# Attention and gated FFN on one core: the order of the work at the end of a sequence and at the start of the kernel

## The chip, the cores and the metric

The kernel runs on one core of a Trainium2 chip. The metric is the device time of an execution in microseconds (us); runs are compared by their median. A core has a tensor engine (PE; its weight loads are shown apart, as PEld), a vector engine (DVE), a scalar engine (ACT), GpSimd (POOL) and a sync engine (SP) that here only starts DMA transfers. Each engine works through its own queue in order, and waits for the others by semaphores. PE writes its results to PSUM, which has eight banks; DVE and ACT read them from there. POOL works on SBUF alone.

## What is computed

Eight sequences (B) of 448 tokens with 12 heads (H) of 64. First attention with normed queries and keys, then a gated feed-forward network on the heads side by side (768 values a token). All data is float32; the weights arrive as float64.

```
q_n, k_n = rmsnorm(q, g_q), rmsnorm(k, g_k)
attn = softmax(q_n @ k_n.T / sqrt(64));  o = attn @ v
x = o, heads side by side: (8 * 448, 768)
xn = x / sqrt(mean(x * x) + 1e-6) * rms_g
out = (silu(xn @ w_gate) * (xn @ w_val)) @ w_out      # 768 -> 1536 -> 768
```

## The kernel before

**Pairs.** The function `safe_scores` works on pairs of heads: `g` counts 48 of them, six to a sequence `b`. The loop over `g` is at the end of the function. For a pair:

- `load_pair`, `load_v`: loads of q, k and v, on SP's queue.
- `squares(g, i)` (L424, L427): ACT squares q (i = 0) or k (i = 1), DVE sums the squares. `rms_qk` (L441, L444): POOL scales the sums `ms` and raises them to the power -1/2 (`rs`). `norm_q` (L448): POOL multiplies q by its `rs`, giving `qn`, a tile with one buffer.
- `turn(g, i)` (L461 to L466): PE transposes `qn` (i = 0) or k (i = 1); ACT brings the first to SBUF with the gains `gqk` as a scale, DVE the second (`qkT`). While the list of feed-forward steps is not empty, their bank is the single bank of `ps_m`.
- `score(g, (0, 1))` and `score(g, (2, 3))` (L476, L480): each fills four banks of `ps_s` (four there are) and ACT takes the exponential of each into `e`, with the key's `rs` as its scale.
- `values(g)` (L501): `e` times v into `av`, also in the `ps_m` bank. `sums(g)` (L512 to L533): the denominators `den`, their reciprocal `rd` on DVE, the product of both to `x`, the square of `x` on ACT, and its sum over the pairs of a sequence, `ss`, on POOL. For g up to 6 (`direct`) `den` is summed by PE from `e`; after that POOL adds the `e` first (L486, L490).

**The norm of a sequence.** `rms_x` sums `ss` over its partitions with PE (`msx`, L546), DVE scales it (L548), POOL takes the power (L550). `norm_x` spreads that power over all partitions with eight matmuls on PE (`rb`, L556), and DVE multiplies the six chunks of `x` by it and by the gain `rg` (L560). `left_factors` makes four sums and differences of quarters of `x` (S1 to S4, L571) for all sequences but the first.

**The feed-forward steps.** The gate and value products of a sequence are made with Strassen's scheme: `quad` does them in seven steps of 12 matmuls (L783), whose results DVE adds (L795), with a tanh on ACT (L802) and two operations on DVE that give `h` (L805, L806). A sum `so` over parts of `h` (L858 to L861) is made for the output product. The first sequence is multiplied plainly (L1008, L1017 to L1020). The output product is `project_out` (L878) for the first two sequences and `out_strassen` (L977) after that. `begin(b, slots)` puts the steps of the output product of sequence b - 1 and of the gate and value products of b into the list `todo`, and `fill` takes them from there between the attention steps of later pairs: a given number, or as many as the share of the slot asks for. Seven steps are left over for the end of the sequence.

**Conversion.** `convert` moves the float64 weights on by one stage each: load (L619), `split` on ACT (L628, L629), `join` on DVE (L634 to L636), one addition on POOL (L672), and a store to scratch memory (L660). It is called at fixed places of the loop and after each step of `fill`; 78 calls do all of it.

**The order.** The engines' queues are filled in the order in which the Python code runs; nothing reorders it. `pe(fn)` counts PE's steps, and `after(n, fn)` hands work to other engines n steps later; n = 0 is right behind the running step. The sum of `squares`, for example, is issued one step later and its power two (for pairs 0 and 1, one). At a sequence's end (`hp == 0`, from g = 12 on) the loop runs: three steps of `todo`, squares of pair g + 2, first turn of g + 1, one step, `rms_x`, one step, `norm_x`, one step, second turn, the rest of the list, `begin`.

Of the kernel before, what the change touches and what calls it, by code (L numbers as in the profile page):

```python
# [8 lines left out]
F32 = mybir.dt.float32  # L9
# [3 lines left out]
ALU = mybir.AluOpType  # L13
# [8 lines left out]
NPAIR = H // 2  # L22
# [3 lines left out]
HT = S // 2  # L26
# [308 lines left out]
def safe_scores(  # L335
# [20 lines left out]
    nc = tc.nc  # L356
# [5 lines left out]
    const, small = pool("c_const", 1), pool("c_small", 4)  # L362
# [5 lines left out]
    ps_s, ps_m, ps_f = pool("c_ps_s", 4, space=PSUM), pool("c_ps_m", 1, space=PSUM), pool("c_ps_f", 3, space=PSUM)  # L368
# [9 lines left out]
    def after(n, fn):  # L378
        due.append((now["t"] + n, fn))

    def pe(fn):
        now["t"] += 1
        fn()
        for item in [d for d in due if d[0] <= now["t"]]:
            due.remove(item)
            item[1]()
# [16 lines left out]
    def load_v(g):  # L403
        if g >= NG:
            return
        b, hp = divmod(g, NPAIR)
        vt = st["v", g] = v_pool.tile([P, 2, NT, D], F32, name="vt")
        nc.sync.dma_start(out=vt.rearrange("p h t d -> p h (t d)"),
                          in_=v[b, 2 * hp:2 * hp + 2].rearrange("h (p t) d -> p h (t d)", t=NT))
# [5 lines left out]
    def squares(g, i):  # L415

        if g >= NG:
            return
        n = 2 * NT
        if i == 0:  # L420
            st["ms", g] = small.tile([P, 2 * n], F32, name="ms")
        ms = st["ms", g]
        sq = tmp.tile([P, n * D], F32, name="sq", tag="sq", bufs=2)
        nc.scalar.activation(sq, st["qk", g][:, i], ACT.Square)  # L424

        def reduce():
            nc.vector.tensor_reduce(out=ms[:, i * n:(i + 1) * n], in_=sq.rearrange("p (n d) -> p n d", d=D), axis=AX_X, op=ALU.add)  # L427

        after(1, reduce)
        if g <= 1:  # L430

            after(1, lambda: rms_qk(g, slice(i * n, (i + 1) * n)))
            if i == 0:
                after(1, lambda: norm_q(g))
        elif i == 1:
            after(2, lambda: rms_qk(g))
            after(2, lambda: norm_q(g))
# [103 lines left out]
    def rms_x(b):  # L541
        assert st["summed", b] == NPAIR - 1
        ss = st.pop(("ss", b))
        ps = ps_f.tile([128, 512], F32, name="msx", tag="f")
        for t in range(NT):
            nc.tensor.matmul(ps[0:P, t:t + 1], lhsT=ss[:, t * P:(t + 1) * P], rhs=ones[:, 0:1], start=True, stop=True)  # L546
        ms = small.tile([P, NT], F32, name="ms4")
        nc.vector.tensor_scalar(ms, ps[0:P, 0:NT], 1.0 / DM, 1e-6, ALU.mult, ALU.add)  # L548
        rs = st["rx", b] = small.tile([P, NT], F32, name="rs4")
        nc.gpsimd.tensor_tensor(rs, ms, mhalf[0:P, 0:NT], ALU.pow)  # L550

    def norm_x(b):
        rs = st.pop(("rx", b))
        ps = ps_f.tile([128, 512], F32, name="rb", tag="f")
        for t in range(NT):
            nc.tensor.matmul(ps[:, t * P:(t + 1) * P], lhsT=rs[:, t:t + 1].to_broadcast([P, 128]), rhs=ident[0:P, 0:P],  # L556
                             start=True, stop=True)
        for hp in range(NPAIR):
            x = st["x", b, hp // 3][:, hp % 3, :]
            nc.vector.scalar_tensor_tensor(x, x, rg[:, hp:hp + 1], ps[:, 0:S], ALU.mult, ALU.mult)  # L560

    def left_factors(b):

        a = st["left", b] = {f"A{r + 1}{h + 1}": st["x", b, h][:, :, r * HT:(r + 1) * HT] for r in range(2) for h in range(2)}
        for h in range(2):
            st.pop(("x", b, h))

        def op(name, first, second, what):

            a[name] = a["A21"] if name == "S3" else s_pool.tile([128, 3, HT], F32, name="xs")  # L570
            nc.vector.tensor_tensor(a[name], a[first], a[second], what)  # L571

        op("S1", "A21", "A22", ALU.add)
        op("S2", "S1", "A11", ALU.subtract)
        op("S3", "A11", "A21", ALU.subtract)
        op("S4", "A12", "S2", ALU.subtract)

    NFP = NFC // 2

# [82 lines left out]
    def convert():  # L662

        n = turn_of["n"]
        if n >= TURNS or not room(1):
            return False
        turn_of["n"] += 1
        if 0 <= n - 4 < len(pieces):
            key = pieces[n - 4][0]
            st[key] = block()  # L670
            lo, top = st.pop(("cv", n - 4))
            nc.gpsimd.tensor_tensor(data(key).bitcast(I32), top, lo, ALU.add)  # L672
        if 0 <= n - 3 < len(pieces):
            st["cv", n - 3] = join(*st.pop(("cv", n - 3)))
        if 0 <= n - 2 < len(pieces):
            st["cv", n - 2] = split(st.pop(("raw", n - 2)))
        if n < len(pieces):
            st["raw", n] = load_raw(pieces[n][1])
        if 0 <= n - 6 < len(pieces):
            keep(pieces[n - 6][0])  # L680
        return True
# [384 lines left out]

    def begin(b, slots):

        if b:
            left_factors(b)  # L1070
        items = (out_items(b - 1) if b else []) + gate_value_items(b)
        part.update(all=float(sum(c for c, *_ in items[:-LEFT])), spent=0.0, slot=0, slots=slots)
        todo.extend(items + (out_items(b) if b == B - 1 else []))
# [14 lines left out]
    for a in range(2):  # L1088
        rows = slice(a * D, (a + 1) * D)
        nc.scalar.dma_start(out=gq[rows, :], in_=g_q.rearrange("(p o) -> p o", o=1))  # L1090
        nc.scalar.dma_start(out=gk[rows, :], in_=g_k.rearrange("(p o) -> p o", o=1))
    for g in range(2):
        load_v(g)
    rg = const.tile([128, NDC], F32, name="rg")
    nc.sync.dma_start(out=rg, in_=moe_rms_g.rearrange("(c p) -> p c", p=128))
    row = const.tile([1, 2, D], F32, name="row")
    nc.sync.dma_start(out=row[:, 0, :], in_=g_q.rearrange("(o d) -> o d", o=1))
    nc.sync.dma_start(out=row[:, 1, :], in_=g_k.rearrange("(o d) -> o d", o=1))
    gqk = const.tile([128, 1], F32, name="gqk")

    def bound():
        nc.vector.scalar_tensor_tensor(gqk, gq, 1.0 / D**0.5, gk, ALU.mult, ALU.mult)

        nc.vector.tensor_scalar(gqk, gqk, SAFE / D, -SAFE / D, ALU.min, ALU.max)
        nc.vector.tensor_tensor(row[:, 0, :], row[:, 0, :], row[:, 1, :], ALU.mult)
        top = const.tile([1, 1], F32, name="top")
        nc.vector.tensor_reduce(out=top, in_=row[:, 0, :], axis=AX_X, op=ALU.max, apply_absolute_value=True)
        nc.vector.tensor_scalar(flag, top, 8.0, SAFE, ALU.mult, ALU.is_gt)


    squares(0, 0)
    pe(idle)
    squares(0, 1)
    pe(lambda: turn(0, 1))
    convert()
    convert()
    bound()
    squares(1, 0)
    squares(1, 1)
    pe(lambda: turn(0, 0))  # L1120
    convert()
    for g in range(NG + 1):
        b, hp = divmod(g, NPAIR)
        load_pair(g + 2)
        if g <= NPAIR:
            pe(lambda: score(g, (0, 1)))
            squares(g + 2, 0)
            squares(g + 2, 1)
            convert()
            pe(lambda: turn(g + 1, 0))  # L1130
            pe(lambda: turn(g + 1, 1))
            if g:
                pe(lambda: values(g - 1))
            load_v(g + 2)
            convert()
            if g:
                pe(lambda: sums(g - 1))
            pe(lambda: score(g, (2, 3)))
            convert()
            continue  # L1140

        if g < NG:
            pe(lambda: score(g, (0, 1)))
        pe(lambda: values(g - 1))
        load_v(g + 2)
        if g == NPAIR + 1:
            pe(lambda: rms_x(0))
            pe(lambda: score(g, (2, 3)))
            pe(lambda: norm_x(0))
        pe(lambda: sums(g - 1))  # L1150
        if g == NPAIR + 1:
            begin(0, 15)
        elif g < NG:
            pe(lambda: score(g, (2, 3)))
        end = hp == 0
        fill(3 if end else None)
        squares(g + 2, 0)
        squares(g + 2, 1)
        pe(lambda: turn(g + 1, 0))
        if end:  # L1160
            fill(1)
            pe(lambda: rms_x(b - 1))
            fill(1)
            pe(lambda: norm_x(b - 1))
        fill(1 if end else None)
        pe(lambda: turn(g + 1, 1))
        if end:
            fill(len(todo))
            begin(b - 1, 16)
        fill()  # L1170
    fill(len(todo))
    for _ in range(3):
# [39 lines left out]
```

## Time and profile before

| | us |
|---|---|
| median of 11 runs (lowest to highest) | 1667.8 (1661.15 to 1669.77) |
| the profiled execution | 1666.87 |
| its span, first to last instruction | 1665.1 |
| PE busy in the span | 1625.8 |
| DVE / ACT / POOL busy | 854.9 / 499.6 / 627.9 |
| mean granted clock of PE | 0.991 |
| DMA traffic | 273.28 MB, 164 GB/s |

The profile is one execution. A line of its time line gives the start and the time of a run of like instructions, the engine, the line of code, the operation, what it writes and reads, and how often; in brackets stands the idle time before it and what ended it. Matmuls overlap, so a PE that is shown as busy may still run slowly; the granted clock tells how much of its full speed it was given. Each float32 matmul of the code is two instructions on PE, a transpose is one.

By the time line the first sequence's attention takes the first 95 us, its gate and value products follow up to about 265, and the seven ends of sequences with `norm_x` in the loop's last part lie at 257, 456, 669, 864, 1069, 1262 and 1460 us. (The first `norm_x`, at 97 us, has a branch of its own.)

### The profile page before, as it was taken

The numbers are of one execution on the slowest core, as the hardware profiler recorded it, in microseconds if no ns is written. First come the engines' busy times: TensorE is split into PE (matmuls) and PEld (weight loads), VectorE is DVE, ScalarE is ACT, GpSimd is POOL, SyncE is SP. The second block draws the span as 40 slices with busy tenths as digits, with TensorE's granted clock in tenths as the row PEclk, the third lists the DMA queues.
The fourth block names the chain that finished last, engine by engine and source line by source line (L and its number), as shares of the span: only waits on it lengthen the run. The fifth ranks groups of instructions, "written<-read, shape, count | busy, mean of one in ns | idle before, by whom it ended". The sixth has DMA issues, their size and how long they took to land.

```text
span 1665.1 us, 21470 instructions
## 1 busy us (share of the span) xinstructions
PE 1625.8 (98%) x7376; PEld 1148.1 (69%) x7376; DVE 854.9 (51%) x1371; ACT 499.6 (30%) x975; POOL 627.9 (38%) x569
## 2 busy tenths in 40 slices
PE   7999998999999999999999999999999999999998
PEld 3444444578855788567875688747876578868984
DVE  6988996366532466425563354623555234432431
ACT  6756563223221232223322222232232222100110
POOL 6777775334423343324432434334343332100000
PEclk9999998999999999999999999999999999999999
DMA  7756673454613766574544555456543564457652
GB/s 200 221 174 199 197 213 92 128 182 150 213 47 114 241 203 219 169 233 146 155 132 125 179 155 154 137 169 203 160 134 95 159 197 133 133 176 238 175 146 70
DMA packets 246443, 273.28 MB, mean 164 GB/s; under 512 B 66356, under 2 KB 243252, under 8 KB 246324
## 3 DMA queue, kind: packets, MB, share of 16 engines
q1 hardware_dynamic: 246004, 271.80, 54.5%
q8 instruction: 61, 1.00, 0.3%
q14 instruction: 58, 0.48, 0.1%
q10 hardware_dynamic: 320, 0.00, 0.0%
HBM read 232.40 MB, written 39.32 MB: 163 GB/s over the span
## 4 chain that ended last, share of the span: by engine, by line
PE 81%; DVE 2%; POOL 2%; issue 0%; ACT 0%; POOLq 0%; DVEq 0%; ACTq 0%
PE ff L783 38%; PE ff L977 18%; PE sc L476 7%; PE av L501 7%; PE ff L878 7%; PE den L512 2%; PE tr L461 1%; POOL rs L444 1%; PE rb L556 1%; PE ff L1008 0%; DVE ms L427 0%; DVE rd L520 0%; POOL rs L550 0%; POOL qn L448 0%; DVE so L859 0%
## 5 line engine op out<-in xcount | busy, mean ns | idle before, releaser
L783 PE MATMUL ff<-x,w 128*128 128x224 f32 x2016 | 410.9, 357 | 0.0
L783 PEld LDWEIGHTS ff<-x,w 128*128 128x128 f32 x2016 | 382.1, 192 | 12.9 <-issue 6.7
L783 PE MATMUL ff<-xs,w 128*128 128x224 f32 x1512 | 308.3, 354 | 0.0
L783 PEld LDWEIGHTS ff<-xs,w 128*128 128x128 f32 x1512 | 283.0, 190 | 5.3 <-issue 5.3
L486 POOL TENSOR_TENSOR es<-e 112x448 f32<-112x448 f32 x82 | 95.2, 1182 | 486.3 <-ACT e L480 486.3
L480 ACT ACTIVATE e<-sc,rs 112x448 f32<-112x448 f32 x384 | 212.0, 636 | 194.8 <-PE sc L476 189.9
L490 POOL TENSOR_TENSOR es<-es,e 112x448 f32<-112x448 f32 x164 | 185.7, 1143 | 85.6 <-ACT e L480 79.2
L520 DVE RECIPROCAL rd<-rd 128x448 f32<-128x448 f32 x41 | 121.1, 2953 | 158.9 <-ACT rd L519 158.9
L977 PE MATMUL ff<-w,h 128*128 128x384 f32 x576 | 191.1, 487 | 0.0
L476 PE MATMUL sc<-qkT 64*112 64x448 f32 x768 | 178.9, 570 | 3.9 <-ACT e L480 3.2
L977 PEld LDWEIGHTS ff<-w,h 128*128 128x128 f32 x576 | 108.5, 190 | 75.5 <-issue 4.0
L501 PE MATMUL av<-e,vt 112*64 112x448 f32 x768 | 154.9, 545 | 0.0
L444 POOL TENSOR_TENSOR rs<-ms,mhalf 112x16 f32<-112x16 f32 (+1 forms) x50 | 143.6, 2872 | 4.2
L476 PEld LDWEIGHTS sc<-qkT 64*112 64x112 f32 x768 | 69.3, 174 | 96.2 <-issue 70.0
L501 PEld LDWEIGHTS av<-e,vt 112*64 112x64 f32 x768 | 50.8, 136 | 95.3 <-issue 71.2
L1008 PE MATMUL ff<-x,w 128*128 128x448 f32 x288 | 114.2, 549 | 0.0
L878 PE MATMUL ff<-w,h 128*128 128x384 f32 x336 | 111.0, 488 | 0.0
L977 PE MATMUL ff<-w,so 128*128 128x384 f32 x324 | 108.6, 488 | 2.0 <-DVE y L938 2.0
L795 DVE TENSOR_TENSOR cc<-ff,u 128x448 f32<-128x448 f32 x84 | 52.4, 623 | 95.2 <-PE ff L783 94.8
L878 PEld LDWEIGHTS ff<-w,h 128*128 128x128 f32 x336 | 63.0, 190 | 44.1 <-issue 3.0
L977 PEld LDWEIGHTS ff<-w,so 128*128 128x128 f32 x324 | 60.5, 190 | 44.7 <-DVE y L938 3.9
L672 POOL TENSOR_TENSOR w<-top,raw 128x384 int32<-128x384 int32 x72 | 77.3, 1085 | 35.0 <-DVE top L636 13.1
(86 smaller groups left out, 1441.7 us busy)
## 6 DMA issues: line engine op xcount, KB each, us to landing
w<-kept SPq DMA_DIRECT2D x552, 192.0 KB, 3.2
w<-kept_o SPq DMA_DIRECT2D x318, 192.0 KB, 2.8
kept<-w SPq DMA_DIRECT2D x96, 192.0 KB, 3.8
qk<-in_q_dram SPq DMA_DIRECT2D x48, 224.0 KB, 3.4
qk<-in_k_dram SPq DMA_DIRECT2D x96, 112.0 KB, 3.8
vt<-in_v_dram SPq DMA_DIRECT2D x48, 224.0 KB, 2.9
raw<-in_moe_w_gate_dram SPq DMA_DIRECT2D x24, 384.0 KB, 4.5
raw<-in_moe_w_val_dram SPq DMA_DIRECT2D x24, 384.0 KB, 4.6
```

The lines of the kernel that those rows point to most:

```text
L444: nc.gpsimd.tensor_tensor(st["rs", g][:, cols], ms, mhalf[0:P, cols], ALU.pow)
L476: nc.tensor.matmul(ps[0:P, 0:S], lhsT=qkT[r, 1, c * P:(c + 1) * P], rhs=qkT[r, 0, :], start=True, stop=True)
L480: nc.scalar.activation(e, ps[0:P, 0:S], ACT.Exp, scale=rs[:, n:n + 1])
L486: nc.gpsimd.tensor_tensor(es, st["e", g, 0, j], st["e", g, 1, j], ALU.add)
L490: nc.gpsimd.tensor_tensor(es, es, st["e", g, c, j], ALU.add)
L501: nc.tensor.matmul(av[j * D:(j + 1) * D, 0:S], lhsT=vt[:, j, c, :], rhs=st["e", g, c, j], start=(c == 0), stop=(c == NT - 1))
L520: nc.vector.reciprocal(rd, rd)
L672: nc.gpsimd.tensor_tensor(data(key).bitcast(I32), top, lo, ALU.add)
L783: nc.tensor.matmul(bank[:, w * HT:(w + 1) * HT], lhsT=wt[:, c * 128:(c + 1) * 128], rhs=x[:, c, :], start=onto is None and w == c == 0, st ...
L878: nc.tensor.matmul(ps, lhsT=st["h", b, fc][:, i * 128:(i + 1) * 128], rhs=data(("wo", b, *block_of(n, fc))), start=(fc == 0), stop=(fc == ...
L977: nc.tensor.matmul(ps, lhsT=a, rhs=data(("wo", b, name, c)), start=first and c == 0, stop=c == NFP - 1, skip_group_check=True)
L1008: nc.tensor.matmul(bank[w][:, 0:S], lhsT=data(key)[:, c * 128:(c + 1) * 128], rhs=st["x", 0, half][:, c, :], start=half == c == 0, stop=ha ...
```

## The change

Ends of sequences:

- The squares of the next pair come after `rms_x`, and the second turn right after them. Before, they came ahead of the first turn.
- `norm_x` comes after the rest of the list and after `begin`. It issues its six scalings two to a step, at 0, 1 and 2 steps, and then S1 to S4 one to a step, at 3 to 6. `left_factors` is merged into it. The first sequence (`b == 0`) still gets all six scalings at once.
- `msx` and `rb` of all sequences but the first use a bank of the scores (`ps_s`) and not one of the products (`ps_f`).

Beginning:

- Pair 2 is loaded ahead of the first values, and its squares are issued before the first scores. The gains' product `gqk` has a function of its own (`gains`), ahead of pair 1's squares; the loads of `rg` and of the gain rows go behind four conversions, and `bound`, which reads those rows, goes to the end of g = 2.
- Both score steps of pair 0 come one after the other, then both turns of pair 1, `load_v(2)` and four conversions. No conversion comes before them (there were three), and g = 1 and g = 2 have one more each.
- `warm` issues 9 and then 3 matmuls of the identity with itself, whose result nothing reads.

```diff
@@ rms_x, norm_x
-        ps = ps_f.tile([128, 512], F32, name="msx", tag="f")
+        ps = (ps_s if b else ps_f).tile([128, 512], F32, name="msx", tag="s" if b else "f")
...
+        def scale(hp):
+            x = xs[hp // 3][:, hp % 3, :]
+            nc.vector.scalar_tensor_tensor(x, x, rg[:, hp:hp + 1], ps[:, 0:S], ALU.mult, ALU.mult)
         for hp in range(NPAIR):
-            x = st["x", b, hp // 3][:, hp % 3, :]
-            nc.vector.scalar_tensor_tensor(x, x, rg[:, hp:hp + 1], ps[:, 0:S], ALU.mult, ALU.mult)
+            if b:
+                after(hp // 2, lambda hp=hp: scale(hp))
+            else:
+                scale(hp)
...
+        for i, args in enumerate((("S1", "A21", "A22", ALU.add), ("S2", "S1", "A11", ALU.subtract),
+                                  ("S3", "A11", "A21", ALU.subtract), ("S4", "A12", "S2", ALU.subtract))):
+            after(NPAIR // 2 + i, lambda args=args: op(*args))
@@ the beginning
+    load_pair(2)
     for g in range(2):
         load_v(g)
...
+    def warm(n):
+        ps = ps_m.tile([128, 512], F32, name="warm", tag="m")
+        for _ in range(n):
+            nc.tensor.matmul(ps[:, 0:128], lhsT=ident, rhs=ident, start=True, stop=True)
     squares(0, 0)
+    warm(9)
     pe(idle)
     squares(0, 1)
     pe(lambda: turn(0, 1))
-    convert()
-    convert()
-    bound()
+    gains()
     squares(1, 0)
     squares(1, 1)
+    warm(3)
     pe(lambda: turn(0, 0))
-    convert()
+    squares(2, 0)
+    squares(2, 1)
     for g in range(NG + 1):
         b, hp = divmod(g, NPAIR)
-        load_pair(g + 2)
+        if g:
+            load_pair(g + 2)
+        if g == 0:
+            pe(lambda: score(0, (0, 1)))
+            pe(lambda: score(0, (2, 3)))
+            for i in range(2):
+                pe(lambda: turn(1, i))
+            load_v(2)
+            for _ in range(4):
+                convert()
+            load_rows()
+            continue
...
             convert()
+            if g <= 2:
+                convert()
+            if g == 2:
+                bound()
@@ the end of a sequence
-        end = hp == 0
-        fill(3 if end else None)
-        squares(g + 2, 0)
-        squares(g + 2, 1)
-        pe(lambda: turn(g + 1, 0))
-        if end:
-            fill(1)
-            pe(lambda: rms_x(b - 1))
-            fill(1)
-            pe(lambda: norm_x(b - 1))
-        fill(1 if end else None)
-        pe(lambda: turn(g + 1, 1))
-        if end:
-            fill(len(todo))
-            begin(b - 1, 16)
+        if hp:
...
+        fill(3)
+        pe(lambda: turn(g + 1, 0))
+        fill(1)
+        pe(lambda: rms_x(b - 1))
+        squares(g + 2, 0)
+        squares(g + 2, 1)
+        pe(lambda: turn(g + 1, 1))
+        fill(len(todo))
+        begin(b - 1, 16)
+        pe(lambda: norm_x(b - 1))
         fill()
```

Between the ends of sequences (`if hp`) the order stays as it was.

More of the change, by code (lines that the diff above doesn't have):

```diff
@@ L553, in norm_x @@
         rs = st.pop(("rx", b))
-        ps = ps_f.tile([128, 512], F32, name="rb", tag="f")
+        ps = (ps_s if b else ps_f).tile([128, 512], F32, name="rb", tag="s" if b else "f")
         for t in range(NT):
@@ L557, in norm_x @@
                              start=True, stop=True)
+        xs = [st["x", b, h] for h in range(2)]
+        def scale(hp):
+            x = xs[hp // 3][:, hp % 3, :]
+            nc.vector.scalar_tensor_tensor(x, x, rg[:, hp:hp + 1], ps[:, 0:S], ALU.mult, ALU.mult)
         for hp in range(NPAIR):
-            x = st["x", b, hp // 3][:, hp % 3, :]
-            nc.vector.scalar_tensor_tensor(x, x, rg[:, hp:hp + 1], ps[:, 0:S], ALU.mult, ALU.mult)
-    def left_factors(b):
-        a = st["left", b] = {f"A{r + 1}{h + 1}": st["x", b, h][:, :, r * HT:(r + 1) * HT] for r in range(2) for h in range(2)}
+            if b:
+                after(hp // 2, lambda hp=hp: scale(hp))
+            else:
+                scale(hp)
+        if b == 0:
+            return
+        a = st["left", b] = {f"A{r + 1}{h + 1}": xs[h][:, :, r * HT:(r + 1) * HT] for r in range(2) for h in range(2)}
         for h in range(2):
@@ L571, in op @@
             nc.vector.tensor_tensor(a[name], a[first], a[second], what)
[L573 to L576, printed above, removed]
+        for i, args in enumerate((("S1", "A21", "A22", ALU.add), ("S2", "S1", "A11", ALU.subtract),
+                                  ("S3", "A11", "A21", ALU.subtract), ("S4", "A12", "S2", ALU.subtract))):
+            after(NPAIR // 2 + i, lambda args=args: op(*args))
     NFP = NFC // 2
@@ L1067, in begin @@
     def begin(b, slots):
-        if b:
-            left_factors(b)
         items = (out_items(b - 1) if b else []) + gate_value_items(b)
@@ L1091, in safe_scores, with gains, load_rows, bound @@
         nc.scalar.dma_start(out=gk[rows, :], in_=g_k.rearrange("(p o) -> p o", o=1))
+    load_pair(2)
     for g in range(2):
         load_v(g)
+    gqk = const.tile([128, 1], F32, name="gqk")
     rg = const.tile([128, NDC], F32, name="rg")
-    nc.sync.dma_start(out=rg, in_=moe_rms_g.rearrange("(c p) -> p c", p=128))
     row = const.tile([1, 2, D], F32, name="row")
[L1097 to L1101, printed above, removed]
+    def gains():
         nc.vector.scalar_tensor_tensor(gqk, gq, 1.0 / D**0.5, gk, ALU.mult, ALU.mult)
         nc.vector.tensor_scalar(gqk, gqk, SAFE / D, -SAFE / D, ALU.min, ALU.max)
+    def load_rows():
+        nc.sync.dma_start(out=rg, in_=moe_rms_g.rearrange("(c p) -> p c", p=128))
+        nc.sync.dma_start(out=row[:, 0, :], in_=g_q.rearrange("(o d) -> o d", o=1))
+        nc.sync.dma_start(out=row[:, 1, :], in_=g_k.rearrange("(o d) -> o d", o=1))
+    def bound():
         nc.vector.tensor_tensor(row[:, 0, :], row[:, 0, :], row[:, 1, :], ALU.mult)
@@ L1131, in safe_scores @@
             pe(lambda: turn(g + 1, 1))
-            if g:
-                pe(lambda: values(g - 1))
+            pe(lambda: values(g - 1))
             load_v(g + 2)
             convert()
-            if g:
-                pe(lambda: sums(g - 1))
+            pe(lambda: sums(g - 1))
             pe(lambda: score(g, (2, 3)))
             convert()
+            if g <= 2:
+                convert()
+            if g == 2:
+                bound()
             continue
@@ L1154, in safe_scores @@
             pe(lambda: score(g, (2, 3)))
-        end = hp == 0
-        fill(3 if end else None)
+        if hp:
+            fill()
+            squares(g + 2, 0)
+            squares(g + 2, 1)
+            pe(lambda: turn(g + 1, 0))
+            fill()
+            pe(lambda: turn(g + 1, 1))
+            fill()
+            continue
+        fill(3)
+        pe(lambda: turn(g + 1, 0))
+        fill(1)
+        pe(lambda: rms_x(b - 1))
         squares(g + 2, 0)
         squares(g + 2, 1)
-        pe(lambda: turn(g + 1, 0))
-        if end:
-            fill(1)
-            pe(lambda: rms_x(b - 1))
-            fill(1)
-            pe(lambda: norm_x(b - 1))
-        fill(1 if end else None)
         pe(lambda: turn(g + 1, 1))
-        if end:
-            fill(len(todo))
-            begin(b - 1, 16)
+        fill(len(todo))
+        begin(b - 1, 16)
+        pe(lambda: norm_x(b - 1))
         fill()
```

## The prediction

> **What bounds the kernel now.** I read the page's busy shares first, then the tensor engine's waits, then the time line round the waits, and last a table of windows for the clock. The first two lines are from the page, the next three from the waits of the tensor engine (who waited for whom: total us, times, longest).
>
> ```profile
> PE 1625.8 (98%) x7376; PEld 1148.1 (69%) x7376; DVE 854.9 (51%) x1371; ACT 499.6 (30%) x975; POOL 627.9 (38%) x569
> PEclk9999998999999999999999999999999999999999
> ...
> PE rb L556 <- POOL rs L550: 18.7, 6, 6.9
> PE tr L461 <- DMA qk<-in_k_dram: 5.6, 1, 5.6
> PE sc L476 <- ACT e L480: 3.2, 1, 3.2
> ```
>
> The tensor engine sets the end: 39 us idle in all, and 18.7 of it in one place, the matmul `rb` of `norm_x`, before six of seven sequence ends. The rest is the beginning. So the change is worth what those gaps are worth. One end, from the time line:
>
> ```profile
> 663.22 0.86 PE L546 MATMUL msx<-ones,ss 128*112 128x1 f32 x8
> ...
> 663.66 2.91 POOL L444 TENSOR_TENSOR rs<-ms,mhalf 112x16 f32<-112x16 f32 x1
> ...
> 664.11 0.16 DVE L548 TENSOR_SCALAR ms<-msx 112x4 f32<-112x4 f32 x1
> ...
> 666.65 1.04 POOL L448 TENSOR_TENSOR qn<-qk,rs 112x512 f32<-112x512 f32 x1
> 667.65 1.00 POOL L550 TENSOR_TENSOR rs<-ms,mhalf 112x4 f32<-112x4 f32 x1
> 668.71 1.81 PE L556 MATMUL rb<-ident,rs 112*128 112x112 f32 x8 [2.26 <-POOL rs L550]
> ...
> 670.32 3.49 PE L783 MATMUL ff<-x,w 128*128 128x224 f32 x12
> ```
>
> The sums of squares are ready at 664.08, but POOL is inside the next pair's power (2.91 us) and then its `qn`; the sequence's own power (1.00) starts 3.4 us late. PE has one product (2.28 us) to cover 4.7.
>
> **What a gap costs beyond its length.** After the gap 12 product matmuls took 3.49 us, where 2.45 is usual. The table of windows shows why (its columns: window, length, busy PE, PEld, DVE, ACT, POOL, granted clock, DMA share, GB/s):
>
> ```profile
> 858.60:863.60 5.00, 2.40 (x13) 2.06 (x12) 0.85 (x3) 0.00 (x0) 4.87 (x3) 1.00 0.41 123
> 863.60:873.60 10.00, 9.99 (x44) 8.87 (x45) 6.87 (x13) 0.97 (x2) 0.00 (x0) 0.83 0.35 98
> ...
> 1069.00:1079.00 10.00, 10.00 (x50) 8.23 (x50) 8.78 (x15) 1.24 (x3) 0.00 (x0) 1.00 0.43 126
> ```
>
> The ten us after the gap at 861 ran at 0.83 of the clock, those after the gap at 1066 at 1.00, with 50 matmuls in place of 44. I measure it from the start of `rb` to the end of the product behind it. Undisturbed (1068.72 to 1071.98) that is 3.26 us; the others take 4.81, 4.93, 4.88 and 4.95, a loss of 1.55, 1.67, 1.62 and 1.69. The first end (257.30 to 263.24, 5.94) loses 2.67. Sum 9.2 us. Waits (6.94, 2.17, 2.26, 2.60, 2.17, 2.60): 18.7. The seventh end (1460) has no gap, since no next pair is prepared there.
>
> [...] By the rows four of five short gaps cost it too: 18.7 + 9.2 = 27.9. [...]
>
> **The ends of sequences, edit by edit.** *Order.* `rms_x` now stands ahead of the next pair's squares, and `turn(g+1, 1)`, the last three items and `begin` stand between it and `norm_x`. POOL gets the small power first: ready 0.03 + 0.16 + 1.0, some 1.5 us after `msx`. PE's cover is a turn (0.38) and three products (3 x 2.28): 7.2 us. The wait goes in all six. At the first end DVE runs behind (its `ms` at 251.95, 4 us after `msx`) with two reductions ahead (1.27); these now follow, so `ms` comes about 250.8 and the power by 252, against a need at 255.1.
>
> *What is late next.* The next pair's reductions, power and `qn` move some 3 us back; they are wanted by `turn(g+2, 0)` a pair later, some 20 us away: nothing, and if that cover went, at most the 4 us of POOL work. The first turn's ACT copy (0.62) must leave the single `m` bank before the second turn, now 3.0 us later instead of 13; the squares (1.14), formerly ahead of it on ACT, are now behind: nothing.
>
> *Scalings and left factors.* The six scalings (0.676 each) go two per step, then one factor operation (0.85) per step. The products that read them come after 18 to 28 output steps of 1.94 to 2.6 us; the factors are complete after seven. Nothing, and the 3.4 us block of factors no longer holds up the last gate's `h`.
>
> *The bank.* `rb` leaves the products' banks and takes one of four score banks until the sixth scaling; the fourth score tile of the next pair must wait for it. DVE's list from the end of `rb`: c12 0.62, two halves 0.77, two `h` 1.24, `so` sums 1.14 (2.28 in odd sequences), six scalings 4.06: 7.8 to 9.0. PE's: 24 output matmuls 7.76 and three score tiles 1.3: 9.0. Just covered; I put 1.0 us in all for it (between 0 and 6).
>
> [...]
>
> **The beginning.** PE's and POOL's rows:
>
> ```profile
> 14.31 1.64 POOL L444 TENSOR_TENSOR rs<-ms,mhalf 112x8 f32<-112x8 f32 x1
> 17.85 0.21 POOL L441 TENSOR_SCALAR ms<-ms 112x16 f32<-112x16 f32 x1 [1.90 <-DVE ms L427]
> 18.14 3.17 POOL L444 TENSOR_TENSOR rs<-ms,mhalf 112x16 f32<-112x16 f32 x1
> 21.39 1.04 POOL L448 TENSOR_TENSOR qn<-qk,rs 112x512 f32<-112x512 f32 x1
> ...
> 19.90 3.82 PE L476 MATMUL sc<-qkT 64*112 64x448 f32 x8 [3.21 <-ACT e L480]
> ...
> 24.66 3.23 PE L501 MATMUL av<-e,vt 112*64 112x448 f32 x16
> ```
>
> From 24.66 on PE is fed (score, turns, values and sums repeat every 11.31 us until 87), so the beginning is worth what the first `values` moves. Before, the scores of pair 1 waited until 19.90 because ACT did pair 2's late squares and a conversion ahead of pair 0's exponentials. Now pair 0's scores run together; ACT, from about 11 us, does eight exponentials (0.55 each), pair 1's scaling (0.63) at about 16, so pair 1's scores fall at 16 to 18. POOL then limits: its list up to 15.95 is the same work; the 1.90 us it waited for pair 2's reductions goes, since pair 2's loads are issued at 5 and not 9 us. So pair 2's `qn` ends at 22.43 - 1.85 = 20.6, two turns (1.0) follow, and `values` starts at 21.6: 3.05 us gained.
>
> Against it: PE idles about 2.5 us before 20.6 and, by the rows above, loses 1.6 of clock. Warming matmuls: 9 and 3, two instructions each; nearest row `rb`, cold 2.05/8 = 0.26 for 112 columns, so 0.29 x 18 = 5.3 us from 1.3 (the identity is done) to 6.7, which moves the first turn from 5.56 and POOL's k power by 0.4, swallowed by its 0.44 us wait before 10.91. On SP pair 2's three loads (1.9 us) pass the two `v` loads, wanted at 21: nothing. The rg and row loads fall behind four weight loads; wanted at about 50 and 95: nothing. Conversions: five instead of seven lie ahead of the first `values`; the two others follow pairs 1 and 2 (DVE 1.3 to 2.7 each) with `bound` (0.6). DVE has 3 us of slack up to there and then little: 9.79 of 10 us busy at 70 to 80. A reciprocal more than 1.35 us late (x done at 68.57, `values` at 69.91) stalls PE. I put 0.5 (0 to 5). Net 3.05 - 1.6 - 0.5 = 0.9.
>
> **Sum.** 27.9 - 1.0 + 0.9 = 27.8 us. The profiled execution took 1666.87 (span 1665.1 and 1.8 outside): 1639.1. The median of the runs lies 0.9 higher: 1640.
>
> **Rivals.** 0.2%, 3.3 us, is about what a measurement can tell here.
> - *As summed*, 1634 to 1646: chance 0.64.
> - *The beginning loses*: the later conversions make the reciprocals late through pairs 2 to 6, up to 5 us: 1640 + 5 = 1645 to 1648. For it the DVE share; against it 2 us of each DVE cycle are waits for POOL that can shift. 0.12.
> - [...] 0.08.
> - *The wait moves to the score bank*: 2.4 us and 1.6 of clock at some ends, half of it back: 1654 to 1660. For it the thin margin (0 to 1.2 us). 0.08.
> - *It doesn't do what it says*: `norm_x` still meets a late power because DVE's `ms` is queued behind evictions; only the clock or the start changes, 1664. Against it 7.2 us of cover. 0.03.
> - [...] 0.05.
>
> So faster 0.92, same 0.03, slower 0.05. The range 1632 to 1652 leaves out the last three and a little beside: 0.18.
>
> **What would show it.** Right: no wait of `rb` for `rs` among the tensor engine's waits; granted clock 1.00 in the ten us after each sequence end; the small power on POOL ahead of the 112x16 one; the scalings in three pairs; first `values` at 21 to 23. Wrong: a score waiting for a scaling (L560's successor), a clock of 0.83 near the ends, `values` waiting for `x` between 40 and 95.

## The result, and the profile after

The changed kernel takes 1641.8 us in the median (1639.48 to 1643.15), the kernel before 1666.19 in the same comparison. The ratio is 0.9851, with a 95% interval of 0.9838 to 0.9864: 24.8 us faster, where the prediction said 27.8. The profiled execution took 1639.78 us with a span of 1638.0, so 27.1 us less than the one shown of before. Lines are numbered anew after the change: L783 is now L793, L977 is L987, `rb` is L558 and the scalings are L565.

First the page's two lines that answer to those of before.

```profile
PE 1618.8 (99%) x7400; PEld 1146.3 (70%) x7400; DVE 862.1 (53%) x1371; ACT 500.5 (31%) x975; POOL 631.8 (39%) x569
...
PEclk9999999999999999999999999999999999999999
```

Then the waits of the tensor engine over 1 us (total us, times, longest).

```profile
PE tr L461 <- POOL qn L448: 3.5, 3, 1.4
PE sc L476 <- ACT e L480: 2.5, 1, 2.5
PE ff L987 <- DVE y L948: 2.0, 3, 0.7
PE den L512 <- ACT e L480: 1.8, 1, 1.8
PE warm L1127 <- POOL ident masks.py:199: 1.4, 1, 1.4
```

The 18.7 us of `rb` waiting for `rs` are gone. A score waited for exponentials in both kernels, but not at the same place: 3.2 us at 19.90 before, with pair 1's scores, and 2.5 us at 53.97 after the change. The end of the third sequence, from the time line, beside the one shown of before:

```profile
651.93 0.85 PE L546 MATMUL msx<-ones,ss 128*112 128x1 f32 x8
...
652.64 0.58 PE L461 MATMUL tr<-ident,qk 112*128 112x112 f32 x4
652.82 0.16 DVE L548 TENSOR_SCALAR ms<-msx 112x4 f32<-112x4 f32 x1
...
653.06 1.02 POOL L550 TENSOR_TENSOR rs<-ms,mhalf 112x4 f32<-112x4 f32 x1 [4.78 <-DVE ms L548]
...
655.45 2.90 POOL L444 TENSOR_TENSOR rs<-ms,mhalf 112x16 f32<-112x16 f32 x1
...
659.89 1.04 PE L558 MATMUL rb<-ident,rs 112*128 112x112 f32 x8
...
661.35 2.45 DVE L565 SCALAR_TENSOR_TENSOR x<-x,rg,rb 128x448 f32<-128x448 f32 x4
...
665.03 0.29 DVE L868 TENSOR_TENSOR so<-h,h 128x128 f32<-128x128 f32 x1
...
665.97 1.27 DVE L565 SCALAR_TENSOR_TENSOR x<-x,rg,rb 128x448 f32<-128x448 f32 x2
...
668.62 1.76 PE L476 MATMUL sc<-qkT 64*112 64x448 f32 x8
```

The small power runs from 653.06 to 654.08, the next pair's large one after it, and `rb` comes at 659.89, 5.8 us after its power is ready. The sixth scaling ends at 667.24, before the next score even starts, so the score bank is free in time. In the ten us behind `rb` the granted clock is 1.00 at all six ends that had a gap; two of these windows (window, length, busy PE, PEld, DVE, ACT, POOL, granted clock, DMA share, GB/s):

```profile
659.90:669.90 10.00, 10.00 (x41) 5.88 (x39) 9.61 (x19) 1.24 (x3) 0.00 (x0) 1.00 0.75 224
850.20:860.20 10.00, 10.00 (x41) 5.90 (x39) 9.49 (x21) 1.71 (x4) 0.00 (x0) 1.00 0.44 126
```

**Where the time went.** The order of PE's attention steps is the same in both kernels from the first `values` on, so the start of each pair's `values` step is a mark that can be compared. The table gives these marks from one profiled execution of each kernel, those of the experiments below included. Pair 2 to 3 lies in the beginning; pair 11 to 12 holds the first sequence end with `norm_x` in the loop; 12 to 47 holds the five others that had a gap.

| kernel | first values at | pair 2 to 3 | 3 to 6 | 6 to 11 | 11 to 12 | 12 to 47 |
|---|---|---|---|---|---|---|
| before | 24.66 | 11.31 | 33.02 | 139.66 | 44.14 | 1168.60 |
| changed | 20.87 | 16.03 | 33.03 | 141.10 | 34.64 | 1148.56 |
| ends_only | 22.58 | 11.31 | 33.03 | 139.27 | 34.82 | 1148.55 |
| order_only | 23.34 | 11.31 | 33.03 | 139.20 | 38.69 | 1148.82 |
| filled_gap | 24.68 | 11.31 | 33.03 | 140.64 | 43.89 | 1161.96 |
| start_only | 21.07 | 16.00 | 34.65 | 139.57 | 43.65 | 1168.64 |
| load_first | 21.01 | 11.88 | 33.03 | 142.91 | 34.87 | 1148.56 |
| no_extra | 21.22 | 11.31 | 33.03 | 140.37 | 34.36 | 1148.55 |
| no_warm | 21.07 | 15.55 | 33.03 | 139.49 | 34.76 | 1148.56 |
| bank_f | 21.15 | 16.07 | 34.72 | 141.93 | 34.22 | 1148.56 |

The change gains 9.5 us at the first end (44.14 - 34.64) and 20.0 at the five others: 29.5. Its first `values` comes 3.8 us earlier, but then 4.7 us are lost between pair 2 and pair 3. That loss is this study's question, beside the clock.

### The profile page after: what moved, and what is told of

It reads as the page before. It is cut to its first block, busy times and chain, and to the rows that moved or that the text cites. A ratio compares the mean times of both kernels' runs of the same rounds, so it can differ in the third digit from the quotient of the medians.

```text
span 1638.0 us, 21517 instructions
## 1 busy us (share of the span) xinstructions
PE 1618.8 (99%) x7400; PEld 1146.3 (70%) x7400; DVE 862.1 (53%) x1371; ACT 500.5 (31%) x975; POOL 631.8 (39%) x569
## 4 chain that ended last, share of the span: by engine, by line
PE 90%; DVE 6%; DMA 2%; POOL 1%; ACT 1%; SPq 0%; issue 0%; POOLq 0%; DVEq 0%; ACTq 0%
PE ff L793 41%; PE ff L987 18%; PE sc L476 9%; PE av L501 8%; PE ff L888 7%; PE den L512 3%; PE ff L1018 2%; PE tr L461 2%; DVE top L646 1%; DVE top L645 1%; DVE top L644 1%; DVE rd L520 1%; DMA raw<-in_moe_w_val_dram 1%; DMA raw<-in_moe_w_gate_dram 0%; POOL rs L444 0%; PE rb L558 0%
## 5 line engine op out<-in xcount | busy, mean ns | idle before, releaser
L793 PE MATMUL ff<-x,w 128*128 128x224 f32 x2016 | 405.7, 353 | 0.0
L793 PEld LDWEIGHTS ff<-x,w 128*128 128x128 f32 x2016 | 378.5, 190 | 12.0 <-issue 7.3
L793 PE MATMUL ff<-xs,w 128*128 128x224 f32 x1512 | 307.9, 353 | 0.0
L793 PEld LDWEIGHTS ff<-xs,w 128*128 128x128 f32 x1512 | 283.4, 190 | 5.3 <-issue 5.3
L987 PE MATMUL ff<-w,h 128*128 128x384 f32 x576 | 191.1, 487 | 0.0
L987 PEld LDWEIGHTS ff<-w,h 128*128 128x128 f32 x576 | 108.1, 190 | 75.5 <-issue 4.0
L987 PE MATMUL ff<-w,so 128*128 128x384 f32 x324 | 108.6, 488 | 2.0 <-DVE y L948 2.0
L987 PEld LDWEIGHTS ff<-w,so 128*128 128x128 f32 x324 | 60.5, 190 | 44.7 <-DVE y L948 3.9
```

The costliest lines, as they stand in the source:

```text
L793: nc.tensor.matmul(bank[:, w * HT:(w + 1) * HT], lhsT=wt[:, c * 128:(c + 1) * 128], rhs=x[:, c, :], start=onto is None and w == c == 0, st ...
L987: nc.tensor.matmul(ps, lhsT=a, rhs=data(("wo", b, name, c)), start=first and c == 0, stop=c == NFP - 1, skip_group_check=True)
```

## The experiments

Each experiment has a median and a ratio to the kernel before, with its 95% interval. A gain or loss in us is the distance of that ratio from 1, times 1666.2.

**The ends alone, and the beginning alone.** `ends_only` has the changed `rms_x`, `norm_x`, `begin` and order at a sequence's end, with the beginning of before; `start_only` the reverse.

> The beginning of before with the changed sequence ends. Theory, from how far each pair's values step moved between the two traces (first values 3.8 us earlier, then 4.7 lost at pair 3 and 1.5 more by pair 11, and 29.5 gained over six ends): the changed beginning as a whole loses some 2.4 us, so this kernel runs 29.5 us under before, near 1637, and beats the changed kernel by 2 to 5. Rival, the losses at pair 3 and pair 10 belong to that one execution: the beginning is worth the 0.9 us of the prediction or more, and this kernel is 1 to 4 us slower than the changed one, 1643 to 1646.

> Before, with the changed beginning alone. Theory, as for ends_only: slower than before by 1 to 4 us, 1667 to 1670, though its first values start 3.8 us earlier; ACT waits for pair 5's q and k near 48 us, and a score step for exponentials near 54. Rival, as predicted: 0.9 us faster, 1664 to 1666, or 3.8 faster if the loss was of one execution, 1662.

`ends_only`: 1637.33 us, ratio 0.9825 (0.9806 to 0.9845), 29.2 us under before. `start_only`: 1673.97 us, ratio 1.0037 (1.0022 to 1.0052), 6.2 us slower. The ends gain what the marks say, the beginning loses: by the difference of the changed kernel and `ends_only` 4.3 us (0.9851 - 0.9825; the two intervals just overlap), alone 6.2. The changed beginning made this kernel slower than it need be, and the sixteen us from pair 2 to pair 3 stand in `start_only`, `no_warm` and `bank_f` too. They are no chance of one execution. The 6.2 us are not all accounted for: the runs of `start_only` lie between 1668.93 and 1677.86 us, and the profiled one, 1669.05, has marks that add up to a loss of only 2.2. No profile shows where the other 4 us went.

**The order alone.**

```diff
-        squares(g + 2, 0)
-        squares(g + 2, 1)
+        if not end:
+            squares(g + 2, 0)
+            squares(g + 2, 1)
         pe(lambda: turn(g + 1, 0))
         if end:
             fill(1)
             pe(lambda: rms_x(b - 1))
+            squares(g + 2, 0)
+            squares(g + 2, 1)
```

> Before, with one edit: at a sequence's end the squares of the next pair come after rms_x, so the small power stands first on POOL. norm_x stays one product behind rms_x, in a product bank, with its six scalings in one block. Theory: order alone takes the wait, since the power is ready 1.2 to 1.5 us after msx and one product covers 2.28; 27 to 29 us under before, 1637 to 1639, and the first end may keep 1 to 3 us of wait because DVE is behind there. Rival: the later place of norm_x and the spread scalings are needed; then half or more of the waits stay and it gains 15 us or less, 1651 or more.

1639.07 us, ratio 0.9834 (0.9813 to 0.9854): 27.7 us under before from these lines. From pair 12 on it is 0.27 us behind `ends_only` (1148.82 and 1148.55). Only the first end keeps a wait:

```profile
250.05 1.02 POOL L550 TENSOR_TENSOR rs<-ms,mhalf 112x4 f32<-112x4 f32 x1 [0.96 <-DVE ms L548]
...
251.12 2.00 PE L556 MATMUL rb<-ident,rs 112*128 112x112 f32 x8 [2.48 <-POOL rs L550]
252.91 3.29 PE L1008 MATMUL ff<-x,w 128*128 128x448 f32 x6
```

There POOL waited for DVE, which is behind with conversions (its `ms` starts at 249.82), as the prediction had it for that end; one product does not cover it. The later place of `norm_x` and the spread of its scalings are together worth that one gap with its clock: `order_only` and `ends_only` differ by 3.9 us from pair 11 to 12 in one execution of each. Their medians are 1.7 us apart, and the intervals overlap.

**The clock by itself.** In before, 8 matmuls of the identity are put into the gap, in a bank of the scores. They compute nothing that is used, and the wait for the power keeps its end.

```diff
             fill(1)
             pe(lambda: rms_x(b - 1))
             fill(1)
+            busy(8)
             pe(lambda: norm_x(b - 1))
```

> Before, with 8 matmuls of the identity with itself (16 instructions, about 1.9 us) put between the product and norm_x, in a score bank, in every sequence end; nothing waits for them. The wait for the power stays as long as it was in sum. By the rows (a gap of 2.2 to 2.6 us costs clock): granted clock 1.00 after the five short gaps, 6.5 us under before, 1659 to 1660, with the first end's long gap still costing its clock. [...]

1661.32 us, ratio 0.9969 (0.9957 to 0.9981): 5.2 us under before (3.2 to 7.2). The time line at the end at 668, and the windows behind the first end, behind this one and behind the next:

```profile
665.37 1.95 PE L1113 MATMUL busy<-ident 128*128 128x128 f32 x16
667.80 1.14 PE L556 MATMUL rb<-ident,rs 112*128 112x112 f32 x8 [0.48 <-POOL rs L550]
668.78 2.45 PE L783 MATMUL ff<-x,w 128*128 128x224 f32 x12
```

```profile
251.00:261.00 10.00, 4.85 (x28) 4.06 (x27) 3.83 (x10) 3.54 (x8) 8.17 (x7) 0.77 0.41 115
...
667.80:677.80 10.00, 10.00 (x49) 8.36 (x50) 8.50 (x15) 0.96 (x2) 0.00 (x0) 1.00 0.92 309
861.00:871.00 10.00, 9.95 (x49) 8.32 (x50) 8.45 (x15) 0.97 (x2) 0.00 (x0) 1.00 0.40 109
```

With 0.38 to 0.84 us of idling left at the five short ends, the clock is 1.00 and the product behind `rb` takes 2.45 us again; the marks from pair 12 to 47 are 6.64 us closer than in before, against 6.53 by the prediction's rows for these ends. The first end keeps a gap of 5.15 us, and its window stands at 0.77. So gaps of 2.17 to 2.60 us can cost clock here.

They do not always cost it. In before the gap at 1066 was spared, 2.17 us long like the one at 453 that was not. In `start_only`, whose ends are those of before, that same end was slow (a gap of 2.16 us, then 3.85 us for the product), and the third end was spared (2.27 us, then 2.45). So it isn't the place in the program that spares a gap; what does was not tried. Nor was the length at which the loss begins: a single gap of 1.80 us in the changed kernel, ending at 183.65, left the clock at 1.00.

**The loss at pair 3.** In the changed kernel the rows of SP, POOL, ACT and PE show what happens. First SP's queue and its longest wait in it (total us, times, longest), with the POOL rows that it waited for:

```profile
36.91 0.38 SPq L629 DMA_DIRECT2D raw<-in_moe_w_val_dram  x1
37.35 0.49 SPq L670 DMA_DIRECT2D kept<-w  x1
42.71 0.37 SPq L629 DMA_DIRECT2D raw<-in_moe_w_val_dram  x1
43.14 0.48 SPq L670 DMA_DIRECT2D kept<-w  x1
43.67 0.42 SPq L397 DMA_DIRECT2D qk<-in_q_dram  x1
44.13 1.24 SPq L400 DMA_DIRECT2D qk<-in_k_dram  x2
...
SPq L629 <- POOL w L682: 5.1, 2, 4.8
...
37.69 2.90 POOL L444 TENSOR_TENSOR rs<-ms,mhalf 112x16 f32<-112x16 f32 x1
40.67 1.04 POOL L448 TENSOR_TENSOR qn<-qk,rs 112x512 f32<-112x512 f32 x1
41.67 2.15 POOL L682 TENSOR_TENSOR w<-top,raw 128x384 int32<-128x384 int32 x2
```

Then ACT (with its idle time and what ended it):

```profile
47.75 0.63 ACT L424 ACTIVATE sq<-qk 112x512 f32<-112x512 f32 x1 [1.91 <-DMA qk<-in_q_dram]
50.03 0.63 ACT L424 ACTIVATE sq<-qk 112x512 f32<-112x512 f32 x1 [1.66 <-DMA qk<-in_k_dram]
...
53.30 2.19 ACT L480 ACTIVATE e<-sc,rs 112x448 f32<-112x448 f32 x4
```

And PE:

```profile
49.67 1.76 PE L476 MATMUL sc<-qkT 64*112 64x448 f32 x8
53.97 3.69 PE L476 MATMUL sc<-qkT 64*112 64x448 f32 x8 [2.54 <-ACT e L480]
58.62 0.60 PE L461 MATMUL tr<-ident,qn 112*128 112x112 f32 x4 [0.95 <-POOL qn L448]
```

The added conversion at the end of pair 2's round loads a weight block at 42.71. SP stood 4.8 us before it, until a POOL addition freed the block's buffer, and that addition was queued behind the power and `qn` of pair 4 (POOL ran them from 37.69 to 41.71). Pair 5's q and k stand behind it, at 43.67. ACT reaches pair 5's squares and waits 3.6 us for them; pair 3's exponentials are behind that, PE's next score needs their banks and waits 2.54, the turn waits 0.95 more, and the score ran at half pace (3.69 us in place of 1.76, clock 0.83 from 50 to 60). In before these loads were issued 5.5 us ahead of pair 2's `values`; here they are 0.2 us behind it (43.67 and 43.50). The rows of before:

```profile
41.79 0.48 SPq L397 DMA_DIRECT2D qk<-in_q_dram  x1
...
47.29 3.23 PE L501 MATMUL av<-e,vt 112*64 112x448 f32 x16
```

In `start_only` and `bank_f` these two waits (2.5 to 2.6 us and 2.1) are followed a little later by slow `values` of pair 3 (4.85 and 4.92 us in place of 3.23): this is where their 34.7 us from pair 3 to 6 come from.

`load_first` (the first of the two diffs) puts the loads of pairs 4 and 5 ahead of the added conversions and changes nothing else; `no_extra` (the second) leaves the added conversions out of pairs 1 and 2.

```diff
-        if g:
+        if g not in (0, 2, 3):
             load_pair(g + 2)
...
             if g <= 2:
+                load_pair(g + 3)
                 convert()
```

```diff
-            if g <= 2:
-                convert()
```

> The changed kernel with one edit: in pairs 1 and 2 the loads of q and k of pair g + 3 stand on SP's queue ahead of the added conversion, not behind it. Theory: the added conversion's weight load waits on SP for a POOL addition that stands behind the next pair's power, and pair 5's loads wait behind it; ACT then waits for pair 5 with pair 3's exponentials behind. With the order turned, pair 3's values come 11.3 us after pair 2's and not 16.0, and the kernel takes 4.7 us less than the changed one, 1637; up to 1.5 more if the later loss near pair 10 goes too. Rival, from the prediction: DVE's added work (two joins of 1.3 to 2.7 us and the bound) makes the lateness; then the gap at pair 3 stays and the time is that of the changed kernel, 1641 to 1642.

> The changed kernel without the added conversions of pairs 1 and 2; the two come later, in the first sequence's feed-forward steps. Both theories of the loss at pair 3 expect it to go here: pair 3's values 11.3 us after pair 2's, and 4.7 us less than the changed kernel, 1637. If the loss is neither (a chance lateness of the loads), 1641 to 1642. Conversions that then come late for the feed-forward steps would show after 100 us, as 1 to 3 us of wait at ACT's or POOL's hands.

`load_first`: 1637.99 us, ratio 0.982 (0.9797 to 0.9843). `no_extra`: 1635.78 us, ratio 0.9814 (0.9793 to 0.9836). The first interval just overlaps that of the changed kernel, 0.9838 to 0.9864, and the second just misses it; the marks decide. From pair 2 to pair 3 they take 11.88 and 11.31 us, where the changed kernel takes 16.03. In `load_first` DVE has all of its added work, and ACT no longer waits for the squares' data:

```profile
38.08 0.47 SPq L397 DMA_DIRECT2D qk<-in_q_dram  x1
38.59 1.31 SPq L400 DMA_DIRECT2D qk<-in_k_dram  x2
42.67 0.38 SPq L629 DMA_DIRECT2D raw<-in_moe_w_val_dram  x1
...
45.66 1.18 ACT L424 ACTIVATE sq<-qk 112x512 f32<-112x512 f32 x2
```

The weight load comes at the same time as before the edit (42.67), held up by the same addition; with q and k ahead of it, this costs PE nothing but the remaining 0.6. So the order on SP's queue makes the loss, and not DVE's work.

**The warming matmuls and the bank.** `no_warm` leaves out `warm(9)` and `warm(3)`; `bank_f` puts `msx` and `rb` back into `ps_f`.

```diff
-    warm(9)
...
-    warm(3)
```

```diff
-        ps = (ps_s if b else ps_f).tile([128, 512], F32, name="msx", tag="s" if b else "f")
+        ps = ps_f.tile([128, 512], F32, name="msx", tag="f")
...
-        ps = (ps_s if b else ps_f).tile([128, 512], F32, name="rb", tag="s" if b else "f")
+        ps = ps_f.tile([128, 512], F32, name="rb", tag="f")
```

> The changed kernel without the 12 matmuls of the identity. Theory: POOL's list sets the first values, so the colder first scores cost little: first values 0 to 1 us later, 1641 to 1643. Rival, the warm clock is what brings the first exponentials early, since ACT waited 0.95 us for the first score: 1.5 to 3 us later, 1643 to 1645.

> The changed kernel with msx and rb back in the products' banks; all else as changed. Theory: the four output steps behind norm_x need two of the three product banks, so the held bank costs nothing: 1641 to 1642. Rival: the held bank stops a product until the sixth scaling, 1 to 3 us at each of six ends with clock lost where it exceeds 2 us: 1648 to 1665.

`no_warm`: 1639.86 us, ratio 0.984 (0.9818 to 0.9862), not to be told from the changed kernel's. Its first score starts at 10.25 and not 9.74, its first `values` at 21.07 and not 20.87; but kernels that do have the warming matmuls have their first `values` at 20.87 to 21.22, so these matmuls are worth nothing that can be told there. POOL's list sets that point, as expected: the turn ahead of it waited for `qn` in both, 1.15 us in the changed kernel and 0.33 in `no_warm`. `bank_f`: 1642.21 us, ratio 0.9851 (0.9826 to 0.9876); from pair 12 on it is equal to the changed kernel to 0.01 us. The bank is worth nothing that can be told.

`no_extra` is the fastest kernel of the study, 31 us under before; from `ends_only`, 29.2 under, the intervals do not part it. Leaving out both the added conversions and the warming matmuls was not tried.

## Why the prediction was right or wrong

**The sum, right in part by luck.** 27.8 was predicted and 24.8 came. The ends carry it, and there the mechanism was right; but two errors of opposite sign are in the closeness. The ends gained 2.3 us more than their 26.9 (by `ends_only`), and the beginning came out 5.2 us worse than its 0.9.

**The ends, right.** Predicted 27.9 less 1.0; measured 29.2 by `ends_only`, 29.5 by the marks. The waits and the clock were summed from the right rows: 6.64 us of clock at the five short ends were recovered by filling the gaps alone, against 6.53. The sum was a little low, by 20.0 - 18.3 = 1.7 at these five ends: each gap cost about 0.3 us more than its idle time and its slow clock, counted from `rb` on. This is not clock: at the end of before that kept its clock, 5.67 us lie between the starts of the two products around `rb` (1064.03 and 1069.70), and without a gap, in `order_only`, 3.23 (652.61 and 655.84). The difference is 2.44, 0.27 more than the wait of 2.17 that the profile gives. At the first end 9.6 was predicted and 9.5 came, though DVE's `ms` came 4.4 us after `msx` began (253.92 and 249.52), where the predicted 250.8 would have been 3.7 after; the cover of 7 us took that.

**The bank, right as covered, its 1.0 us too dear.** PE waited for no scaling at any end. DVE's list took 6.5 us from the product behind `rb` on (660.77 to 667.24), not 7.8 to 9.0, and POOL's next power and `qn` (655.45 to 659.47) were over when it began, as the order had it. The first of the `so` sums took 0.29 us, as it did in before at 682.29 with POOL idle; while POOL was adding there (654.94 to 659.56), the sums at 656.27 and 657.35 took 1.05 and 1.22.

**The beginning, wrong in sign.** Predicted 0.9 gained, measured 4.3 lost in the pair of kernels that differ in it, 6.2 alone. Step by step:

- *The first `values`*: predicted 21.6, came at 20.87. POOL's wait for pair 2's reductions went, as the step had it. But the 3.05 us were taken from one execution of before; kernels with the old beginning have their first `values` at 22.58 to 24.68, those with the new at 20.87 to 21.22. The gain lies between 1.4 and 3.8, and the profiled execution of before was at the far end. The nine first warming matmuls took 4.2 us in the changed kernel and not 5.3, and delayed no turn.
- *The clock there, 1.6 lost*: PE's gap before the turn was 1.15 us and not 2.5, and the clock stood at 1.00 from 20 to 30.
- *The later conversions, 0.5 on DVE (0 to 5)*: this step failed. The conversions cost 4.7, near the upper bound, but by another way. The prediction followed their DVE work and named the reciprocals; it left out that each also issues a weight load and a store on SP, that the load waits for a POOL addition, and that pair 5's q and k stand behind it. "On SP ... nothing" had looked only at pair 2's loads and the gain rows. `load_first` settles it: with the DVE work kept and the SP order turned, 4.15 of the 4.7 us from pair 2 to pair 3 come back.

**Of the rivals**, the one called "The beginning loses" came nearest in size (up to 5 us), with the wrong cause. "It doesn't do what it says" and the wait at the score bank fell with the rows above, and the kernel did not come out slower.

**What stays open.** From pair 6 to 11, in the first sequence's feed-forward steps, profiled executions took from 139.2 to 142.9 us. With the old beginning it was 139.2 to 140.6, with the new 139.5 to 142.9. In the changed kernel ACT waited there 3.31 us for a weight block's landing (to 180.18) and PE 1.8 us for the exponentials behind it (to 183.65). In `load_first`, which has the longest, ACT waited 2.28 us for such a block and PE 2.13 us behind it, and the clock stood at 0.91 from 168 to 188. One execution of each doesn't tell whether the beginning does this or chance does. The 4 us of `start_only` that no profile shows are open too.

## What to carry to other kernels

A wait of the engine that set the end was worth more than its length here: 2.17 to 2.60 us of waiting cost 1.6 us of clock behind it at four of five places. So look at the granted clock in the window behind each gap before you sum. The cure here was three lines: the short item that is waited for goes ahead of the long one that isn't. When a step is moved, list what it puts on every queue, the DMA queue above all: here a weight load that waited 4.8 us for its buffer held up the loads behind it, the one that hurt belonged to another pair (pair 5's q and k), and 4.7 us were lost.

## What was not expected of the hardware

PE idling of 2.17 to 2.60 us took the granted clock to 0.83 over the next ten us at four of five places in before, 1.6 us each, and in `start_only` the product behind the gap was slow at four of five again, but not at the same four. Idling of 0.38 to 0.84 us left it at 1.00 at all five. These waits cost PE about 0.3 us more than the length that the profile gives them, even where the clock stayed whole.

In the beginning the whole scheme of PE, ACT, DVE and POOL kept its pitch of 11.31 us from pair to pair to 0.02 us in every kernel that was not disturbed, while the first `values` moved by 2 us between kernels with the same beginning. Part of that is the loads: ACT squared pair 2's k at 16.41 in before and at 15.59 in `ends_only` (first `values` at 24.66 and 22.58), as soon as it had landed. But `order_only` squared it at 16.35 and came to its first `values` at 23.34; there the first score of pair 1 took 2.58 us where it took 3.82 in before, behind a wait of 0.37 and not 3.21. What makes that difference was not followed.
